# A gated mix of linear attention and a GEGLU block: the state from a Gram product, the read-out folded into one matrix, and the stages reordered

## The chip, the cores and the metric

One core of one Trainium2 chip. The time is the device time of one launch in microseconds, median of several runs. The three batches of experiments ran on three different chips, so across batches I compare the ratios to the kernel before. A profile is one further execution; its span is 1.7 us shorter than the timed run of the same kernel. The chain of a profile is the work that ended last, followed back at each step to what released it.

## The reference

```
g = sigmoid(x . gate_w)                         # x: 2048 x 640
q, k, v = heads(x @ wqkv)                       # 32 heads of 20
pq, pk = phi(q), phi(k)                         # t+1 above zero, exp(t) below, + 1e-6
kv = sum over tokens of pk^T v ;  z = sum over tokens of pk
a = ((pq kv) / (pq . z + 1e-6)) @ wo
b = (gelu(x @ w_gate) * (x @ w_up)) @ w_down    # 640 -> 1728 -> 640
out = g * a + (1 - g) * b
```

## The kernel before

The tokens are 16 row tiles of 128, in four quarters of 512. Everything runs through 8 PSUM banks. K and V come from one projection per row tile. A per-head state with a column for z is accumulated in two banks, each row tile is read out against it and divided, and both branches meet in one PSUM accumulation with wo and w_down.

```python
    def phase_B(st):                      # K, V and the gate column of a row tile
        ...
        for (lo, hi) in chunks:           # 512, 508 and 261 columns
            ps = ps_tile("ps_kv")
            for dk in range(ND):
                nc.tensor.matmul(ps[:, 0 : hi - lo], lhsT=xT[q][:, dk, sl * P : (sl + 1) * P],
                                 rhs=wkv[:, dk, lo:hi], ...)
        ...
        if pend_kv:
            phase_KV()                    # five outer products pk^T [v, 1] of the tile before
    ...
    def phase_D(st):                      # six matmuls pq x state, then
        ...                               # divide: two reciprocals, two multiplies on VectorE
    ...
    phase_A(0)
    phase_A(1)
    filler(3)
    ...
    for i in range(NT):
        if i < NF:
            phase_E(0, i)                 # one FFN feature tile of quarter 0
        phase_D(i)
    for q in range(NQ):
        if q > 0:
            for ft in range(NF):
                phase_E(q, ft)
        for sl in range(4):
            phase_F(4 * q + sl)           # 5 matmuls with wo and 14 with w_down, per half of 320 columns
```

## Time and profile before

| | before |
|---|---|
| median (lowest to highest) | 288.85 us (287.9 to 289.32), 16 runs |
| span of the profile | 287.1 us |
| TensorE share of the chain | 98% |
| VectorE busy | 114.6 us, 40% |

The prediction shows the busy table and the chain. The mean of a group counts a matmul from issue to result, and matmuls overlap, so what a matmul costs is the distance to the next one. The groups below, from the list of groups by shape (busy us, mean ns, idle time before), are the ones that the change takes out or replaces:

```profile
L208 PE MATMUL ps_kv<-wkv,xT 128*128 128x512 bf16 x80 | 19.9, 379 | 0.0
L239 PE MATMUL kv_ps<-v_ext,pk 128*128 128x147 bf16 x64 | 7.9, 228 | 0.0
L271 PE MATMUL nd_ps<-kvz,pqT 128*128 128x147 bf16 x16 | 3.6, 227 | 0.0
L293 DVE TENSOR_TENSOR o_sb<-nd_ps,rg 128x380 bf16<-128x380 f32 x16 | 8.8, 553 | 0.0
```

The second and third are the state and a part of the read-out: small matmuls whose only purpose is to build and read per-head sums. The fourth is VectorE's division: 553 ns for 380 columns, where the FFN's product takes 691 ns for 512 columns. The difference is 1.05 ns a column, the pace that the prediction calls 0.96 GHz.

### The profile page before, as it was taken

What the parts mean: (1) busy time and instruction counts of PE and PEld (TensorE: products, weight loads), DVE (VectorE), ACT (ScalarE), POOL (GpSimd) and SP (SyncE); (2) the same over time, 40 slices, a digit from 0 to 9 for tenths busy, and PEclk for the clock granted to TensorE, in tenths of its full rate; (3) what the DMA queues carried; (4) which work ended last, traced back from release to release, by engine and by line L of the source; (5) the groups of instructions that cost most, each with busy time, mean ns of one, the idle gap of its engine ahead of it and who ended that gap; (6) DMA issues with size and microseconds to landing.
All of it is one profiled execution on the core that took longest, in us unless ns stands there. A gap on an engine that the chain in (4) does not pass through costs nothing.

```text
span 287.1 us, 4265 instructions
## 1 busy us (share of the span) xinstructions
PE 281.4 (98%) x1705; PEld 159.9 (56%) x1705; DVE 114.6 (40%) x287; ACT 87.1 (30%) x181; POOL 6.8 (2%) x24
## 2 busy tenths in 40 slices
PE   7999999999999999999999999999999999999994
PEld 3656556554455556776444577644457754445773
DVE  0755445359978888501322301132330112332010
ACT  3555556555542212101222210123221013222100
POOL 8100000000000000000000000000000000000000
PEclk9999999999999999999999999999999999999999
DMA  7999990000013433601000000100000010000001
GB/s 225 302 186 330 348 352 10 2 0 0 2 23 69 68 72 59 96 32 48 0 0 0 2 23 25 47 0 0 2 0 23 25 46 0 2 0 0 25 24 45
DMA packets 31027, 18.04 MB, mean 63 GB/s; under 512 B 20960, under 2 KB 29728, under 8 KB 31008
## 3 DMA queue, kind: packets, MB, share of 16 engines
q1 hardware_dynamic: 29696, 16.96, 22.2%
q10 hardware_dynamic: 1312, 0.82, 0.9%
q8 instruction: 13, 0.21, 0.3%
q14 instruction: 6, 0.05, 0.0%
HBM read 10.57 MB, written 2.62 MB: 46 GB/s over the span
## 4 chain that ended last, share of the span: by engine, by line
PE 98%; ACT 1%; DVE 0%; issue 0%; DVEq 0%
PE ps_acc L339 21%; PE ps_g L310 20%; PE ps_u L314 20%; PE ps_kv L208 15%; PE ps_acc L336 8%; PE ps_q L194 7%; PE kv_ps L239 2%; PE ps_gu L322 2%; PE kv_ps L112 1%; ACT xT L171 1%; PE kv_ps L352 0%; PE nd_ps L279 0%; PE nd_ps L281 0%; PE nd_ps L273 0%; PE nd_ps L275 0%; PE nd_ps L271 0%
## 5 line engine op out<-in xcount | busy, mean ns | idle before, releaser
L339 PE MATMUL ps_acc<-wd,hT 128*128 128x320 bf16 x448 | 66.1, 299 | 0.0
L314 PE MATMUL ps_u<-xT,wu 128*128 128x512 bf16 x260 | 64.6, 379 | 0.0
L310 PE MATMUL ps_g<-xT,wg 128*128 128x512 bf16 x260 | 64.6, 379 | 0.0
L318 DVE TENSOR_TENSOR hT<-ps_u,gl 128x512 bf16<-128x512 f32 x52 | 35.9, 691 | 62.4 <-PE ps_u L314 61.6
L317 ACT ACTIVATE gl<-ps_g 128x512 bf16<-128x512 f32 x52 | 31.0, 597 | 87.7 <-PE ps_g L310 85.7
L339 PEld LDWEIGHTS <-hT 128*128 128x128 bf16 x448 | 43.8, 98 | 17.1
L208 PE MATMUL ps_kv<-wkv,xT 128*128 128x512 bf16 (+2 forms) x240 | 45.9, 344 | 0.0
L314 PEld LDWEIGHTS <-wu 128*128 128x128 bf16 x260 | 25.4, 98 | 30.7
L310 PEld LDWEIGHTS <-wg 128*128 128x128 bf16 x260 | 25.0, 98 | 27.4
L345 DVE TENSOR_SCALAR o_out<-ps_acc,omg_all 128x320 bf16<-128x320 f32 x16 | 8.8, 551 | 68.0 <-PE ps_acc L339 68.0
L208 PEld LDWEIGHTS <-xT 128*128 128x128 bf16 x240 | 22.9, 97 | 19.9
L342 ACT ACTIVATE o_out<-ps_acc,omg_all 128x320 bf16<-128x320 f32 x16 | 8.4, 527 | 64.8 <-PE ps_acc L339 64.8
L336 PE MATMUL ps_acc<-wo,oT 128*128 128x320 bf16 x160 | 27.0, 299 | 0.0
L184 DVE TENSOR_SCALAR phi_m<-phi_e 128x512 bf16<-128x512 bf16 (+2 forms) x54 | 13.8, 256 | 25.9 <-ACT phi_e L182 25.1
L194 PE MATMUL ps_q<-xT,wq 128*128 128x512 bf16 (+1 forms) x110 | 22.5, 360 | 0.8 <-ACT xT L171 0.8
L336 PEld LDWEIGHTS <-oT 128*128 128x128 bf16 x160 | 15.6, 98 | 6.5
L182 ACT ACTIVATE phi_e<-ps_kv 128x512 bf16<-128x512 f32 (+1 forms) x32 | 14.0, 437 | 13.7 <-PE ps_kv L208 13.6
L194 PEld LDWEIGHTS <-wq 128*128 128x128 bf16 x110 | 10.6, 97 | 11.3 <-issue 1.1
L187 DVE SCALAR_TENSOR_TENSOR pk<-ps_kv,phi_m 128x512 bf16<-128x512 f32 (+1 forms) x32 | 15.7, 492 | 2.2
L182 ACT ACTIVATE phi_e<-ps_q 128x512 bf16<-128x512 f32 (+1 forms) x22 | 12.2, 558 | 10.6 <-PE ps_q L194 10.6
L187 DVE SCALAR_TENSOR_TENSOR pqT<-ps_q,phi_m 128x512 bf16<-128x512 f32 (+1 forms) x22 | 14.1, 643 | 0.7
L293 DVE TENSOR_TENSOR o_sb<-nd_ps,rg 128x380 bf16<-128x380 f32 (+1 forms) x32 | 14.2, 486 | 0.0
(52 smaller groups left out, 109.5 us busy)
## 6 DMA issues: line engine op xcount, KB each, us to landing
out_dram<-o_out SPq DMA_DIRECT2D x16, 160.0 KB, 1.8
wd<-in_B_w_down_dram SPq DMA_DIRECT2D x1, 2080.0 KB, 13.2
wkv<-in_A_wqkv_dram SPq DMA_DIRECT2D x2, 800.0 KB, 9.1
wg<-in_B_w_gate_dram SPq DMA_DIRECT2D x1, 1440.0 KB, 9.6
wu<-in_B_w_up_dram SPq DMA_DIRECT2D x1, 1440.0 KB, 11.9
wo<-in_A_wo_dram SPq DMA_DIRECT2D x1, 800.0 KB, 11.6
x_sb<-in_A_x_dram SPq DMA_DIRECT2D x2, 320.0 KB, 4.4
wg<-in_B_w_gate_dram SPq DMA_DIRECT2D x1, 640.0 KB, 5.2
```

Of the source, the lines that this page charges most:

```text
L182: nc.scalar.activation(out=e[:, :width], in_=ps[:, :width], func=ACT.Exp)
L184: nc.vector.tensor_scalar(out=m[:, :width], in0=e[:, :width], scalar1=1.0, scalar2=EPS, op0=ALU.min, op1=ALU.add,)
L187: nc.vector.scalar_tensor_tensor(out=dst, in0=ps[:, :width], scalar=0.0, in1=m[:, :width], op0=ALU.max, op1=ALU.add,)
L194: nc.tensor.matmul(ps[:, 0:tw], lhsT=wq[:, dk, j * P : (j + 1) * P], rhs=xT[q][:, dk, t0 : t0 + tw], start=(dk == 0), stop=(dk == ND - 1),)
L208: nc.tensor.matmul(ps[:, 0 : hi - lo], lhsT=xT[q][:, dk, sl * P : (sl + 1) * P], rhs=wkv[:, dk, lo:hi], start=(dk == 0), stop=(dk == ND - 1),)
L293: nc.vector.tensor_tensor(out=o_sb[:, hlo : hlo + hn, :], in0=ndv[:, :, 0:Dh], in1=rg[:, 0:hn, :].to_broadcast([P, hn, Dh]), op=ALU.mult,)
L310: nc.tensor.matmul(psg[:], lhsT=wg[:, dk, ft * P : (ft + 1) * P], rhs=xT[q][:, dk, :], start=(dk == 0), stop=(dk == ND - 1))
L314: nc.tensor.matmul(psu[:], lhsT=wu[:, dk, ft * P : (ft + 1) * P], rhs=xT[q][:, dk, :], start=(dk == 0), stop=(dk == ND - 1))
L317: nc.scalar.activation(out=gl[:], in_=psg[:], func=ACT.Gelu_apprx_tanh)
L318: nc.vector.tensor_tensor(out=hT[:, ft, :], in0=psu[:], in1=gl[:], op=ALU.mult)
L336: nc.tensor.matmul(acc[:, 0:HALF], lhsT=oT[q][:, dk, sl * P : (sl + 1) * P], rhs=wo[:, dk, cs], start=(dk == 0), stop=False)
L339: nc.tensor.matmul(acc[:, 0:HALF], lhsT=hT[:, ft, sl * P : (sl + 1) * P], rhs=wd[:, ft, cs], start=False, stop=(ft == NF - 1))
```

## The change

The intent is to do less on TensorE. K'V with V = X Wv is (K'X) Wv, so the V projection is dropped and a Gram product G = X' phi(K) is accumulated instead, 640 x 640 in five banks at a time. The state is then one small product, and because it does not depend on the token it is multiplied into wo once (M). Each token's division is done on phi(Q) itself, by a row sum z that two fp32 matmuls (one per half of the columns) have copied to all partitions. The stages are reordered (FFN of quarter 0 first), the half-full 14th feature tile is stored twice so that two 64-row matmuls can run side by side, and the warm-up has 7 matmuls instead of 11. The core of the diff, with cuts:

```diff
-    def phase_D(st):
-        nc.tensor.matmul(nd0[:, 0 : 7 * HC], lhsT=pq_lhs(0), rhs=kvz[0][:, 0 : 7 * HC], ...)
-        ...                                              # five more, then the division
+    def phase_G(st, hh):
+        for ct in range(ND):
+            nc.tensor.matmul(g_ps[hh, ct][:, 0:HALF], lhsT=x_sb[q][:, sl, ct * P : (ct + 1) * P],
+                rhs=pk[st][:, hh * HALF : (hh + 1) * HALF], start=(st == 0), stop=(st == NT - 1))
+    def phase_Z(st):                                     # zacc += pk, fp32, 640 columns, VectorE
+    def phase_KV(glo, ghi):                              # 120 x 120 blocks of Wv^T G, masked to heads
+    def phase_M():                                       # state x wo, six groups of heads
+    def phase_D(st):
+        nc.vector.tensor_tensor(out=prod[:], in0=pq[st][:], in1=zrep[:], op=ALU.mult)
+        nc.vector.tensor_reduce(out=den[:], in_=prod[:]..., axis=AX.X, op=ALU.add)
+        ...                                              # + eps, times e^-gate, reciprocal
+        nc.vector.tensor_tensor(out=v, in0=v, in1=rg[:].to_broadcast([P, H, Dh]), op=ALU.mult)
+    def half_pair(st, first):                            # two 64-row matmuls in place of one padded tile
+    ...
+    for st in range(NT): phase_K(st)
+    ...                                                  # Q with G, two passes, then M
+    for ft in range(2, NF):
+        phase_E(1, ft)
+        if ft - 1 < NT:
+            phase_D(ft - 1)
```

## The prediction

> **What bounds the kernel now.** I read the page's busy table and slices first, then the chain that ended last.
>
> ```profile
> PE 281.4 (98%) x1705; PEld 159.9 (56%) x1705; DVE 114.6 (40%) x287; ACT 87.1 (30%) x181; POOL 6.8 (2%) x24
> PE   7999999999999999999999999999999999999994
> PEclk9999999999999999999999999999999999999999
> DMA  7999990000013433601000000100000010000001
> PE 98%; ACT 1%; DVE 0%; issue 0%; DVEq 0%
> ```
>
> TensorE is busy in every slice at full clock and is 98% of the chain, so the span is the length of the matmul stream plus two ends. DMA is quiet after the fifth slice. VectorE is 40% busy on average, but its slices (0755445359978888501322...) reach eight and nine tenths in the middle: that average hides the engine that could become the next bound.
>
> Busy time of a matmul is latency (379 ns for 512 columns), so I take the spacing from the chain in order of time:
>
> ```profile
> 19.54 2.71 PE ps_kv L208 x15
> 22.59 2.71 PE ps_kv L208 x15
> 64.67 14.03 PE ps_q L194 x65
> 83.72 1.08 PE ps_g L310 x5
> 86.24 1.08 PE ps_g L310 x5
> 266.16 1.90 PE ps_acc L339 x14
> 268.74 1.90 PE ps_acc L339 x14
> ```
>
> Line by line: 14.03 / 65 = 0.216 us for 512 columns. An output half takes 268.74 - 266.16 = 2.58 us for 19 matmuls, 0.136 us for 320 columns. A K/V row tile takes 3.05 us, of which 0.34 is five outer-product matmuls. An FFN feature tile with its attention tile takes 2.52, of which 2.16 is the FFN, so the attention read-out is 0.36.
>
> Added up: 540 FFN matmuls x 0.216 = 116.5; Q, 100 x 0.216 = 21.6; K/V and state, 16 x 3.05 = 48.7; read-out, 16 x 0.36 = 5.7; output, 608 x 0.136 = 82.6. The sum is 275.1. The timeline has the last matmul issue end near 283.5 and the first useful stretch start near 9.3 with 10 small matmuls (1.1) done before: 274.2 + 1.1 = 275.3. The method closes to 0.2 us.
>
> For VectorE I took start-to-start times from its timeline, since operations that do not depend on each other overlap:
>
> ```profile
> 66.63 0.28 DVE L184 TENSOR_SCALAR phi_m<-phi_e 128x512 bf16<-128x512 bf16 x1
> 66.95 0.69 DVE L187 SCALAR_TENSOR_TENSOR pqT<-ps_q,phi_m 128x512 bf16<-128x512 f32 x1
> 67.56 0.29 DVE L184 TENSOR_SCALAR phi_m<-phi_e 128x512 bf16<-128x512 bf16 x1
> 83.48 0.69 DVE L318 TENSOR_TENSOR hT<-ps_u,gl 128x512 bf16<-128x512 f32 x1 [0.36 <-PE ps_u L314]
> 84.08 0.37 DVE L287 TENSOR_SCALAR dtmp<-nd_ps,en 128x19 f32<-128x19 f32 x2
> ```
>
> The operation of 0.69 us lets the next one start after 0.60 to 0.61, which is 512 elements at one per 0.96 GHz cycle plus about 0.07. For 320 columns I get 0.40, for 640 columns 0.73. The short min/add of 320 columns is about 0.15 when the next operation is independent. So phi on 320 columns is 0.55.
>
> **What the Trainium skill says.** (1) "VectorE: DVE Perf Modes", section "The perf-mode tier table": with fp32 operands tensor_tensor runs at one element per cycle, and tensor_reduce always does. The one-per-cycle pace agrees with the 0.69 us row; no run yet has the SBUF-only 640-column forms. (2) "ScalarE: Activation LUTs", section "What ACT_TABLE_LOAD costs": about 1283 ns for the load; the trace has 1283 ns for each of its two loads. (3) "TensorE: Matmul & The Clock Gate", section "Weight-path perf modes": the fast weight load needs 128 weight columns, and its LDWEIGHTS section gives P/1.2 ns otherwise, 100 ns for 120. The trace has only 128-column loads, so no run shows it. (4) "TensorEngine Tiling (Array Packing)", section "Key Properties": two tiles of 64 rows can run in parallel, but changing the mode drains the array. No row here shows that either.
>
> **The change part by part.** The intent is algebra: K'V becomes (K'X)Wv, so the V projection disappears but the Gram product x'phi(k) appears; the per-head state is multiplied into wo once (M), so the read-out matmuls disappear; normalisation uses a replicated row sum z on VectorE. Stages are reordered: FFN of quarter 0 first, then K, Q with G, FFN 1, output 0 and so on.
>
> TensorE after, with the same spacings (the built instruction order has exactly these counts):
> - FFN, 540 matmuls, unchanged: 116.5. The page's busiest lines are untouched.
> - K 160, Q 160 and G 160 matmuls of 320 columns: 480 x 0.136 = 65.3, in place of 21.6 + 48.7 + 5.7 = 76.0. This is the main saving: -10.7. V's 51,200 columns are replaced by G's 51,200, so that part is neutral; what goes is the state outer products and the read-out, 12,096 columns each, and short-matmul overhead.
> - Output: 16 x 2 x 18 = 576 matmuls x 0.136 = 78.3 in place of 82.6, as the half-full 14th feature tile is packed as two 64-row tiles. Those are 32 matmuls: 2.2 if every two run together, 4.4 if not; I take 3.0. Net -1.3.
> - New: row-sum in fp32, estimate 1.1 (four passes of 320 columns, twice; an assumption, not a trace row); KV 30 matmuls of 120-column weights, estimate from the skill's load figure 0.1 each = 3.0; M 12 x 0.136 = 1.6. Together +5.7.
>
> Sum: -10.7 - 1.3 + 5.7 = -6.3 us. With nothing else, 288.8 becomes 282.5, or 2.2% less. That sits almost on the 2% line (283.0), so small waits decide.
>
> **What the moved work does to VectorE.** From the start of K to the end of FFN 1 VectorE has: 64 phi x 0.55 = 35; 15 row-sum adds x 0.73 = 11; 13 of 16 normalisations (product, reduce and multiply, each 640 columns: 3 x 0.73, plus reciprocal 0.3 and a small one 0.12 = 2.6) = 34; FFN evictions 15 x 0.60 = 9; copies of G and M, 12 x 0.40 = 5; small ones 2. That is 96 us beside some 65.3 + 1.1 + 3.0 + 1.6 + 29.1 = 100 us of matmuls. So VectorE is nearly the bound for 100 us, where before it had room.
>
> By stage: K has 16 x 1.1 of phi and six adds (4.4) = 22 against 21.8 of TensorE, starting some 2 us late because the last gelu tile and the table load (1.28) sit in front of it. G then takes five of eight PSUM banks, so those must be evicted first: I count a wait of 1. In Q with G (first half) 1.28 per row tile on VectorE against 1.36: about 0.5 to refill. In the second half the scheduler puts about 14 of the 640-column operations beside ten phi: 18 us of VectorE against 14 of TensorE, mostly taken by three spare banks, but VectorE arrives about 2 us late at the end of G. There is the worst spot: G's copies, then KV, kvt, M's 12 evictions are a serial chain through a queue that also holds two normalisations, with only one FFN tile (2.2 us) between each. Queueing the operations in the built order gives M finished about 2.7 us later than its matmuls alone would. FFN 1 afterwards has about 26 us of VectorE work per 25 of TensorE and up to four tiles of slack: no wait. The start has 7 warm-up matmuls in place of 11: perhaps 0.5 of half-clock. Waits: 1 + 0.5 + 2.7 + 0.5 = 4.7; since one wait gives VectorE time to catch up for the next, I take 2.8.
>
> **The rivals.** (A) VectorE really becomes the bound. For: the sum above is 96 of 100, and a little more per operation (dependent neighbours cost their full duration, 0.82 instead of 0.73 by the same line) adds 8 or 9 us. Against: TensorE can run ahead, and the normalisations are spread. Then 290 to 295. (B) The waits are hidden: the order interleaves two normalisations, and banks in the FFN give slack. Then 281 to 283. (C) Weights arrive late at the start, since gate and up weights are now needed first. FFN 0 uses 0.33 MB per 2.16 us, about 150 GB/s, and the page shows 225 to 352 GB/s there, so I expect at most 0.5.
>
> **Range and chances.** 282.5 + 2.8 = 285.3 us. The stall terms are worth 0 to 8, the packed half tiles and KV about 1.5 either way: 281.0 to 290.0 holds it 8 times in 10. Faster by over 2% needs stalls under 0.5: 0.27. Within 2% (283.0 to 294.6): 0.68. Slower: 0.05.
>
> **What would show it.** Right: TensorE still over 93% of the chain, VectorE near 90% from about 40 to 140 us, the longest TensorE idle time at kvt and M, output periods of 18 x 0.136 = 2.44 us. Wrong: TensorE idle of over 8 us on VectorE (A), practically none (B), KV spacings of 55 ns, or a fall of the granted clock after the gaps.

## The result, and the profile after

The changed kernel takes 281.04 us (280.7 to 281.17, 8 runs) against 288.85. A ratio is the mean time of one kernel's runs over that of the other's of the same rounds, so it is not quite the ratio of these medians: 0.9733, 95% interval 0.9719 to 0.9748. That is 7.8 us less, faster by more than 2%. I had forecast 285.3, 3.5 us less. The measured time lies at the very edge of my range (281.0 to 290.0), the gain is more than twice what I forecast, and I had given a gain of over 2% a chance of 0.27 only.

The page of the changed kernel (busy us, share of the span, instructions; then busy tenths in 40 slices; then the chain):

```profile
PE 273.6 (98%) x1711; PEld 163.9 (59%) x1711; DVE 146.2 (52%) x323; ACT 80.8 (29%) x172; POOL 2.8 (1%) x10
PE   7999999999999999999999999999999999999994
DVE  1233279999978999999993133330112334010010
PEclk9999999999999999999999999999999999999999
PE 98%; ACT 0%; DVE 0%; issue 0%; DVEq 0%
```

VectorE's row stands at seven tenths or more for 16 slices, as forecast, and yet it has 0% of the chain. TensorE is still 98%. The chain in order of time (start, length, what) gives the stages:

```profile
35.54 1.08 PE ps_gu L159 x5
36.62 21.85 PE ps_k L197 x160
...
101.09 2.72 PE ps_G L226 x20
103.81 1.08 PE ps_g L159 x5
...
142.58 1.77 PE ps_acc L363 x13
145.02 1.77 PE ps_acc L363 x13
```

The output now has a period of 145.02 - 142.58 = 2.44 us per half instead of 2.58. The stages K, Q with G in two passes, FFN 1 and output 0 begin at 36.62, 58.47, 80.41, 103.81 and 136.25 us. The windows view, cut at those times, shows stretch and length, then busy us and instructions of TensorE, its weight loads, VectorE, ScalarE and GpSimd, the clock and the DMA:

```profile
36.62:58.47 21.85, 21.85 (x163) 15.54 (x161) 20.77 (x65) 16.48 (x47) 0.00 (x0) 1.00 0.85 251
58.47:80.41 21.94, 21.94 (x163) 15.51 (x161) 19.74 (x54) 7.76 (x21) 0.00 (x0) 1.00 0.01 1
80.41:103.81 23.40, 23.40 (x176) 16.80 (x174) 22.37 (x59) 8.66 (x22) 0.00 (x0) 1.00 0.14 25
103.81:136.25 32.44, 32.41 (x170) 15.65 (x168) 32.08 (x65) 11.61 (x22) 0.00 (x0) 1.00 0.28 64
136.25:156.57 20.32, 20.32 (x154) 14.27 (x152) 12.75 (x24) 2.70 (x5) 0.00 (x0) 1.00 0.36 67
```

VectorE is busy for 94.96 of 99.63 us from K to the end of FFN 1, and TensorE hardly waits in any of these stretches. Taking the matmuls away from each stretch (0.1358 us for 320 columns, 0.2158 for 512, both from the chains) leaves 0.1 to 0.2 us in the first Q pass, 0.1 in the second and 0.6 in FFN 1: about 0.9 us of waits and restarts in all. Of the 0.6, M waits 0.4 and two groups of matmuls behind the 120-column ones take 1.19 us instead of 1.08.

The whole difference can be booked by lengths in the two chains:

| part | before | after | change |
|---|---|---|---|
| FFN, 540 matmuls | 116.6 | 116.6 | 0 |
| K, V, Q, state and read-out; after: K, Q and G | 76.2 | 65.3 | -10.9 |
| output | 82.6 | 81.3 | -1.3 |
| row sum 1.07, state product 0.54 + 1.05, M 1.63 | | 4.3 | +4.3 |
| waits and restarts of TensorE from K to FFN 1 | 0 | 0.9 | +0.9 |
| time before the stream, less useful work done in it | 8.2 | 7.5 | -0.7 |
| tail after the last matmul issue | 3.54 | 3.49 | -0.05 |

The sum is -7.75, to rounding the span's 287.1 - 279.3. The row "before the stream" takes a time at which the stream runs without gaps (9.29 and 9.64 us) and subtracts the first-quarter matmuls already done at the later pace (10 and 20 of 256 columns, 0.109 each). Both are read from one profile each, and the start varies between executions, as the next section shows.

### The profile page after: what moved, and what is told of

Its sections match the earlier page's. It is cut to its first block, busy times and chain, and to the rows that moved or that the text cites. A ratio compares the mean times of both kernels' runs of the same rounds, so it can differ in the third digit from the quotient of the medians.

```text
span 279.3 us, 4308 instructions
## 1 busy us (share of the span) xinstructions
PE 273.6 (98%) x1711; PEld 163.9 (59%) x1711; DVE 146.2 (52%) x323; ACT 80.8 (29%) x172; POOL 2.8 (1%) x10
## 4 chain that ended last, share of the span: by engine, by line
PE 98%; ACT 0%; DVE 0%; issue 0%; DVEq 0%
PE ps_g L159 20%; PE ps_acc L363 20%; PE ps_u L159 20%; PE ps_acc L360 8%; PE ps_q L197 8%; PE ps_k L197 8%; PE ps_G L226 8%; PE ps_gu L159 2%; PE warm_ps L119 1%; PE ps_acc L346 1%; PE ps_m L303 1%; PE ps_kv L274 1%; PE tp_x L141 0%; PE ps_z L251 0%; ACT xT L144 0%; DVE o_out L376 0%
## 5 line engine op out<-in xcount | busy, mean ns | idle before, releaser
L159 PE MATMUL ps_g<-xT,wg 128*128 128x512 bf16 (+1 forms) x270 | 64.8, 372 | 0.9 <-ACT xT L144 0.9
L360 PE MATMUL ps_acc<-m_all,pqT 128*128 128x320 bf16 x160 | 27.0, 300 | 0.0
L197 PE MATMUL ps_q<-wqk,xT 128*128 128x320 bf16 x160 | 26.6, 299 | 0.0
L226 PE MATMUL ps_G<-pk,x_all 128*128 128x320 bf16 x160 | 26.4, 299 | 0.0
L197 PE MATMUL ps_k<-wqk,xT 128*128 128x320 bf16 (+1 forms) x160 | 22.0, 300 | 0.0
L185 ACT ACTIVATE phi_e<-ps_q 128x320 bf16<-128x320 f32 x32 | 14.0, 437 | 26.4 <-PE ps_q L197 22.8
L360 PEld LDWEIGHTS <-pqT 128*128 128x128 bf16 x160 | 15.3, 98 | 7.3 <-issue 1.1
L226 PEld LDWEIGHTS <-x_all 128*128 128x128 bf16 x160 | 15.5, 97 | 6.3 <-issue 0.2
L190 DVE SCALAR_TENSOR_TENSOR pq<-ps_q,phi_m 128x320 bf16<-128x320 f32 x32 | 15.4, 482 | 0.3
L190 DVE SCALAR_TENSOR_TENSOR pk<-ps_k,phi_m 128x320 bf16<-128x320 f32 x32 | 14.4, 485 | 0.0
```

What stands on the lines that cost most here:

```text
L159: nc.tensor.matmul(ps[:, t0 : t0 + tw], lhsT=w[:, dk, ft * P : (ft + 1) * P], rhs=xT[q][:, dk, t0 : t0 + tw], start=(dk == 0), stop=(dk == ...
L185: nc.scalar.activation(out=e[:, :width], in_=src, func=ACT.Exp)
L190: nc.vector.scalar_tensor_tensor(out=dst, in0=src, scalar=0.0, in1=m[:, :width], op0=ALU.max, op1=ALU.add,)
L226: nc.tensor.matmul(g_ps[hh, ct][:, 0:HALF], lhsT=x_sb[q][:, sl, ct * P : (ct + 1) * P], rhs=pk[st][:, hh * HALF : (hh + 1) * HALF], start= ...
L360: nc.tensor.matmul(acc[:, 0:HALF], lhsT=pqT[q][:, dk, ts], rhs=M["sb"][:, dk, cs], start=(sl == 0 and dk == 0), stop=False)
```

## The experiments

Twelve runs in three batches, one of them the changed kernel unaltered; each batch has its own runs of the kernel before.

### Where the start comes from

First, more warm-up in the changed kernel:

```diff
-    NWARM = 7
+    NWARM = 11
```

> The changed kernel with 11 warm-up matmuls instead of 7 and nothing else. Theory T (TensorE's stream plus its start sets the time): the four extra cold matmuls of 0.43 us run before the first transpose and push the start back. The x tile had landed by about 4.1 us and the warm-up ended at 4.42, so four more end near 6.1: 1.7 us later, of which up to 0.5 may be won back because the second x tile is waited for less. Expected 282.2 to 282.8 us, ratio to before about 0.978. Rival R1 (the start is set by when x and the first gate weights land, the warm-up being hidden): within 0.3 us of 281.0. Rival of my prediction (fewer warm-up matmuls cost half-clock time): slightly faster than 281.0.

Measured: 281.49 us (281.34 to 282.28), ratio 0.9749 (0.9734 to 0.9763). The timeline of TensorE shows the shift. First the changed kernel:

```profile
4.21 1.27 PE L141 MATMUL tp_x<-ident,x_all 128*128 128x128 bf16 x10
9.48 2.32 PE L159 MATMUL ps_u<-xT,wu 128*128 128x512 bf16 x10
```

and with eleven:

```profile
1.25 4.88 PE L119 MATMUL warm_ps<-zeros_bf 128*128 128x512 bf16 x11 [1.25 <-DVE zeros_bf L86]
5.92 0.99 PE L141 MATMUL tp_x<-ident,x_all 128*128 128x128 bf16 x10
10.94 2.11 PE L159 MATMUL ps_u<-xT,wu 128*128 128x512 bf16 x9
```

The transposes are 1.7 us later and the first up-projection 1.46, and the profiled span is 1.3 us longer. The timed runs are only 0.45 us longer, and the interval overlaps that of the changed kernel. The direction is against my forecast (fewer warm-ups would cost half-clock time); its size stays between 0.4 and 1.3 us. One source of scatter is visible: the ten transposes took 1.27 us in the changed kernel's profile and 0.87 in another profile of the same kernel (the control below). The warm-up matmuls before them come every 0.43 us and later ones of the same size every 0.216, so the transposes probably fall where the pace changes. In the eleven profiles of the changed kernel and its variants with seven warm-up matmuls, K begins anywhere from 36.09 to 37.11 us; with eleven warm-up matmuls it begins at 37.87. Up to 1 us of any difference between two spans below can thus be the start, so stages are compared by their lengths.

Then the reverse, on the kernel before:

```diff
-            nc.tensor.matmul(t[:], ...)  # NWARM per bank, 8 in all, and filler(3) later
+            # NWARM - b per bank, 7 in all, and no filler
```

> The kernel before with 7 warm-up matmuls instead of 11 (four and three, no filler between the transposes and the first projection). T: the first transposes no longer wait for the fillers that end at 6.08 us; x landed near 4; so 0.7 to 1.7 us less: 287.2 to 288.1 us. If the 0.7 us earlier start of the changed kernel comes from its other load order (gate weights first, all on one queue) instead, no change: 288.6 to 289.0, or a little slower because the clock is not warm yet.

Measured: 287.51 us (287.32 to 289.08) against 288.92, ratio 0.9961 (0.9941 to 0.998), so 1.1 us by the ratio (0.6 to 1.7). The kernel before gains about as much from the warm-up alone as the changed kernel's start did, so this part of the gain needs nothing of the algebra: the fillers of the kernel before ran until 6.08 us, and without them the transposes begin at 4.28.

### What the paired half tile is worth

```diff
-            for lo in (0, FL):           # the 64 rows stored twice
+            # stored once, rows 64 to 127 zero, as before
-            for ft in range(NF - 1):
+            for ft in range(NF):         # 14 full tiles; half_pair removed
```

> The changed kernel with the half-full 14th feature tile padded with zeros as before (32 more 128-row matmuls of 320 columns in the groups, no pairs of 64-row matmuls). T: 32 x 0.136 = 4.35 us in place of the 4 x 0.76 = 3.04 that the chain shows for the pairs: plus 1.3 us, 282.3. If the pairs had cost a drain that eats their gain: within 0.3 us of 281.0. If eight banks claimed at once cost a wait in output stages: faster than 281.0.

Measured: 282.57 us (282.25 to 282.77), ratio 0.978 (0.9767 to 0.9792): 0.47% of 288.9, or 1.4 us, as counted. Eight matmuls of 64 rows take 0.65 us in the chain, against 1.09 for eight full ones: the pairs do run side by side.

### What the banks do

The padded kernel can live with seven PSUM banks, so it serves to take one away:

```diff
-tc.tile_pool(name="psum", bufs=8, ...)
+tc.tile_pool(name="psum", bufs=7, ...)
```

> The same padded kernel with seven PSUM banks instead of eight (it no longer needs eight at once). While G holds five, two spare ones stay for Q instead of three. T says VectorE's lag is absorbed only by the bank lead, so taking one away must show: waits of TensorE on VectorE or ScalarE in the Q and G stages, 2 to 8 us slower than the padded kernel with eight. Rival R2 (VectorE simply keeps up, banks do not matter): within 0.5 us of it.

Measured: 284.95 us (284.26 to 285.2), ratio 0.9859 (0.9845 to 0.9874), 2.4 us slower than the padded kernel with eight (both in one batch). From the start of K to the end of G it takes 69.3 us instead of 67.2. VectorE appears in the chain:

```profile
55.70 0.73 DVE zacc L245
58.23 0.89 DVE pk L190 x2
...
87.78 0.82 DVE prod L324
```

These are two places: the end of K, where G claims five banks, and the second pass, where the row sum takes banks from Q. VectorE's work is nearly the same (144.4 us busy against 143.4). So TensorE's freedom from VectorE in the changed kernel is a matter of bank lead. With eight, 0.9 us of waits and restarts remain; with seven there are some 2 us more.

### The weights of 120 columns

```diff
-kp[0 : gw[g], off : off + gw[g]], lhsT=wv[:, ct, GW * g : GW * g + gw[g]],
+kp[0 : lw, off : off + gw[g]], lhsT=wv[:, ct, GW * g : GW * g + lw],     # lw = min(128, rest)
```

> The changed kernel, with the state matmuls' weights widened from 120 to 128 columns (the eight extra output rows are never read). The chain shows 0.083 us for each of these 30 matmuls where 120 columns alone would take 0.053. T with the fast weight load of the skill: 25 of them fall to about 0.055: minus 0.7 us, 280.3, and the weight loads of this line from 135 ns to about 98 as in the other lines. If the 0.083 is the short matmul's own floor: no change.

Measured: 281.11 us (280.69 to 281.34), ratio 0.9736 (0.9715 to 0.9757): no change, against my expectation. The groups by shape, first the changed kernel, then the widened one:

```profile
L274 PE MATMUL ps_kv<-g_sb,wv 128*120 128x120 bf16 x25 | 1.7, 218 | 0.0
L274 PEld LDWEIGHTS <-wv 128*120 128x120 bf16 x25 | 1.7, 135 | 0.2
```

```profile
L275 PE MATMUL ps_kv<-g_sb,wv 128*128 128x120 bf16 x25 | 1.6, 216 | 0.0
L275 PEld LDWEIGHTS <-wv 128*128 128x128 bf16 x25 | 1.5, 98 | 0.3
```

The loads became shorter, 135 to 98 ns, but the matmuls' pace did not move. My 0.083 us was a misreading: I had taken it from stage lengths and given the state product a wait that belongs to M. The chain has 20 of them in 1.05 us, 0.053 each, which is their 120 columns. The longer load is hidden behind the matmuls.

### Less and more work on VectorE

Less: the product and the replicated row sum in bf16.

```diff
-prod = work.tile([P, D], FP32, ...)      zrep = consts.tile([P, D], FP32, ...)
+prod = work.tile([P, D], BF16, ...)      zrep = consts.tile([P, D], BF16, ...)
```

> The changed kernel with the normaliser's product and the replicated row sum in bf16 instead of fp32, which makes 16 of VectorE's 640-column products about 0.33 us shorter, 5 us of VectorE's 95 between 36 and 136 us. T (VectorE is not on the path): 280.6 to 281.1, no change beyond the 0.4 us that the state product M waited for VectorE. Rival R3 (VectorE's load still costs something, hidden in small gaps): 1 us faster or more.

Measured: 281.13 us (280.83 to 281.4), ratio 0.9738 (0.9717 to 0.9758). VectorE's busy time fell from 146.2 to 141.2 us and the time did not change. VectorE is full but not on the path.

More: one, then two further 640-column products per normalisation.

```diff
+        for _ in range(1):                # 2 in the second run
+            junk = work.tile([P, D], FP32, name="junk", bufs=1)
+            nc.vector.tensor_tensor(out=junk[:], in0=pq[st][:], in1=zrep[:], op=ALU.mult)
```

> The changed kernel with one more 640-column fp32 product in each of the 16 normalisations (a result nobody reads): 16 x 0.73 = 11.7 us more on VectorE, about 9.5 of it before the end of FFN 1. T: VectorE has 99.6 - 94.9 = 4.7 us idle between 36.6 and 136.2, plus some 4 us of bank lead, so this dose lands near the edge: 281 to 284 us. My prediction's account, that waits of about 3 us already exist, would have it 9 us slower or more: 290.

Measured: 282.16 us (281.98 to 282.41), ratio 0.9774 (0.9755 to 0.9794): 1.1 us more than the changed kernel for 11.7 us of extra VectorE work. The windows, cut at this run's own stages, show where it went (FFN 1 and output 0):

```profile
104.15:136.74 32.59, 32.23 (x165) 15.66 (x168) 32.35 (x63) 11.62 (x22) 0.00 (x0) 1.00 0.25 57
136.74:157.55 20.81, 20.60 (x153) 14.29 (x152) 20.72 (x38) 2.17 (x4) 0.00 (x0) 1.00 0.22 43
```

FFN 1 is 0.15 us longer, output 0 is 0.5 longer; the other 0.33 us between the spans lie before K, in the start. In output 0 VectorE's time rose from 12.75 to 20.72 us: the normalisations of later quarters slid behind FFN 1, where they are not needed yet.

> The same with two more products in each normalisation: 23.4 us more on VectorE. T: the slack of about 8 us is used up and the rest shows nearly one to one, 288 to 296 us, with VectorE at 99% from K to FFN 1 and TensorE idle on it. If VectorE's work could still be pushed behind the output stages: under 284.

Measured: 290.6 us (289.3 to 290.82), ratio 1.0051 (1.0018 to 1.0084), 9.6 us more. FFN 1 still ends on time (output 0 starts at 136.6 us), and most of the loss comes after output 0, where FFN 2 waits for a bank that VectorE has not emptied. From the page of this run, the granted clock in 40 slices; from the list of waits (who, for whom: us in total, times, longest); and from the chain, the first five matmuls after the wait:

```profile
PEclk9999999999999999999999968999999999999999
PE ps_g L159 <- DVE o_out L379: 4.9, 1, 4.9
170.32 2.29 PE ps_g L159 x5
```

From K to the end of output 0 the changed kernel has 119.95 us and VectorE is busy for 107.7, so 12.2 us are free. 11.7 more fit, nearly. 23.4 more exceed it by 11.2, which looks like the 9.6 that are seen, but the trace books the profile's 9.8 us otherwise. The start is 0.5 us later and output 0 takes 1.05 more. Then six groups of FFN 2 run on free banks, and TensorE waits 0.73 and 4.86 us. After that gap the granted clock fell: the next three groups of five take 2.29, 2.13 and 1.35 us in the chain instead of 1.08, which is 2.5 us more. So 5.6 us are waits in FFN 2, 4.9 of them directly for VectorE; the slower clock behind the gap was not in my account. The time at which VectorE's surplus becomes a wait is set by the free banks as well, so the 12.2 us are a rough mark and not a sharp limit.

### The same kind of work, in K only

```diff
+            nc.vector.tensor_tensor(out=m[:, :width], in0=m[:, :width], in1=zf[:, :width], op=ALU.add)
         # in phi, only for the second half of K: 16 adds of 320 columns
```

> The changed kernel with one extra fp32 add of 320 columns in phi of K's second half, in front of the operation that frees the PSUM bank: 16 x 0.40 = 6.4 us more on VectorE, all of it between 36 and 59 us. That is little more than half the dose of the run with one extra product per normalisation, which cost about 1 us. Theory T (what matters is the last moment by which VectorE's work must be done: for the normalisations it is the end of output stage 0, for K it is the moment G claims five banks, which it only just meets now): TensorE waits 4 to 6.5 us on VectorE around 50 to 62 us, time 285 to 287.5. Rival (any VectorE work is absorbed as long as the total fits): under 282.2.

Measured: 282.43 us (282.24 to 282.71), ratio 0.9787 (0.977 to 0.9804), 1.8 us above the unaltered kernel in the same batch. Less than I expected. The trace tells why: the scheduler, which orders each engine's instructions when the kernel is built, moved the row-sum adds behind K. The first starts at 64.6 us; in the changed kernel it starts at 44.5, and five have run before VectorE's last tile of K (60.46 us). So K's net load rose by 2 to 3 us and not by 6.4. K itself takes 21.85 us as in the changed kernel: TensorE waits nowhere in it. From the start of K to the end of G this run takes 68.36 us and the changed kernel 67.19, so 1.2 us are lost in Q with G, whose order changed too; the rest of the 1.8 lies before K, in the start. That K is less forgiving than the normalisations fits these figures, but the test does not show it.

### The state product and M without FFN tiles between

```diff
-    phase_D(0); phase_E(1, 0); phase_KV(2, NG); phase_E(1, 1); phase_M()
+    phase_KV(2, NG); phase_M(); phase_D(0); phase_E(1, 0); phase_E(1, 1)
```

> The changed kernel with the state products and M placed directly behind G, without the two FFN tiles between them. In the changed kernel this chain (copies of G, state product, mask, M, its evictions) costs TensorE 0.5 us of waiting, where I had forecast 2.7. T: the two FFN tiles hide it; without them TensorE waits for the copies of G (done 1.5 us after G ends), for the mask and for the evictions: 2 to 4 us more, 283 to 285. If the chain were short in itself: within 0.5 of 281.0.

Measured: 282.61 us (282.48 to 282.91), ratio 0.9794 (0.9775 to 0.9814), 2.0 us above the unaltered kernel. The two waits below make 1.5 of it; between the two profiles the rest is the start (K begins at 36.70 instead of 36.22 us). TensorE's timeline now has the waits (in brackets: idle before, and for whom):

```profile
104.75 0.27 PE L274 MATMUL ps_kv<-g_sb,wv 128*120 128x120 bf16 x2 [0.87 <-DVE g_sb L235]
107.16 1.40 PE L303 MATMUL ps_m<-wo_g,kvt 120*120 120x320 bf16 x8 [0.62 <-DVE kvt L282]
```

The chain through VectorE is real. In the changed kernel two FFN tiles lie over it.

### Control and a faster version

> The changed kernel unaltered, as control for the run below on the same chip: 281.0 us, ratio 0.973.

Measured: 280.64 us (280.59 to 281.63), ratio 0.9732 (0.971 to 0.9754).

```diff
-ones_f fp32; rhs=zacc[:, cs]
+ones_f bf16; the last row-sum add writes a bf16 tile zb; rhs=zb[:, cs]
-dma(out=out2[st * P : (st + 1) * P, :], in_=o_out[:])
+# for the last row tile: two DMAs, one per half
```

> Attempt at a faster version: the row sum's last add writes bf16, so that its broadcast takes 2 bf16 matmuls in place of 2 fp32 ones whose four passes take 1.07 us in the trace: 2 x 0.136, minus 0.8 us. And the last output tile leaves in two halves, so that only the second half is written after the last eviction: minus 0 to 0.2. T (TensorE's stream sets the time): 280.0 to 280.3. If waits elsewhere fill the gap: 281.

Measured: 280.06 us (280.03 to 280.26), ratio 0.9705 (0.969 to 0.972). The outputs are right. It is 0.6 us below the control on the same chip; the single times do not overlap, the intervals of the ratios do, so it is faster than the kernel before beyond doubt and than the changed kernel probably. TensorE's timeline shows the row sum, first changed, then this one:

```profile
84.34 1.24 PE L251 MATMUL ps_z<-zacc,ones_f 128*128 128x320 f32 x4
85.41 0.84 PE L226 MATMUL ps_G<-pk,x_all 128*128 128x320 bf16 x5
```

```profile
84.33 0.45 PE L252 MATMUL ps_z<-zb,ones_f 128*128 128x320 bf16 x2
84.62 0.84 PE L226 MATMUL ps_G<-pk,x_all 128*128 128x320 bf16 x5
```

From its start to the next group 1.07 us became 0.29. The split of the last output was not run alone, but the tail after the last matmul issue is 3.2 us in this profile, where the changed kernel and its variants have 3.5. Together that is 1.0 us against the changed kernel's profile, which has the same start, and 0.6 against the control's, where K begins 0.4 us earlier.

## Why the prediction was right or wrong

**The method: right.** Spacing times count gave 268.8 us for TensorE's new stream; without waits the changed kernel's chain gives 267.5. The main saving (-10.7 forecast, -10.9 measured) and the output (-1.3 and -1.3) were right, the output with some luck: the 3.0 us for the paired half tiles was a guess between 2.2 and 4.4 (0.65 and 0.11 us, four times, were measured), as the 1.1 for the row sum was an assumption (1.07). The pace for 640 columns on VectorE held too: the product and the reduction take 0.81 to 0.82 us each, and about 0.73 from start to start in the chain of the run with two extra products. TensorE stayed the bound, and rival A, VectorE as the bound, did not come. Rival C, late weights, did not show either: the stream ran from 9.64 us on without a gap. (I had read the page's first slices as 225 to 352 GB/s; the third shows 186, still above the 150 needed.)

**"New: ... Together +5.7": mis-sized.** It measures 4.3. The whole error is the state product, 3.0 forecast and 1.6 measured. I priced it by how long a weight load lasts, when the load is overlapped and the pace is set by the columns that stream. The run with 128-column weights shows that the load's length has no effect here. The prediction had named the sign, "KV spacings of 55 ns", and that sign came (53 ns).

**"The start has 7 warm-up matmuls in place of 11: perhaps 0.5 of half-clock": wrong in sign.** The start gained 0.7 in the two profiles. The warm-up stood in front of the transposes and x had already arrived. The timeline of the kernel before showed this (fillers until 6.08 us, while x's first load, issued at 0.81, took 3.6 us to land), and I did not look at what the fillers delayed. Both warm-up runs agree in direction, the one on the kernel before clear of noise.

**"Waits: 1 + 0.5 + 2.7 + 0.5 = 4.7 ... I take 2.8": the step that failed most.** Leaving the start aside, 0.9 us was measured. Rival B was right, and three things were wrong in mine.

- At the end of K, I had VectorE too late, as I read the trace, by one 0.73 us add: the add stands between the last tiles of K, after those whose banks G needs first. The wait came out at 0.2 instead of 1. That it is close is shown by the run with seven banks, which does wait there.
- "VectorE arrives about 2 us late at the end of G": it was 0.34 us late, since the first copy of G starts at 104.15 and G's last matmul is issued by 103.81. My running sum let VectorE begin that stretch of work 1.0 us after a Q tile ended on TensorE, and the trace has it begin 0.7 us before (first product at 86.07, that Q tile's end 86.78). With the chain starting 1.6 us earlier, M waited 0.4 us instead of 2.7. I had also put M's 12 evictions into VectorE's queue, where the code gives every second one to ScalarE. The run without FFN tiles in between shows the chain itself.
- "VectorE is nearly the bound": its load was right (96 us forecast, 94.96 measured), but I set the deadline at the end of FFN 1. Normalisations of later quarters may finish as late as output 0, and the run with one extra product shows 11.7 us more being absorbed for 1.1, the start's scatter included. A sum of 96 out of 100 was not an engine near its limit, because much of the work could move.

In numbers: the forecast change of -3.5 was -6.3 + 2.8. Measured, -6.3 is -7.9 (the state product and rounding), and +2.8 is +0.9 for waits and -0.7 for the start, with -0.05 at the tail.

What stays open: the exact size of the start's part (0.4 to 1.3 us), and how the row sum adds and G's banks would fare under a heavier K, as the scheduler rearranged that test.

## What to carry to other kernels

Price a matmul by the columns it streams and count them before and after; that part of a forecast was good to one or two microseconds of 280. Before charging a wait to an engine that will be nearly full, ask for each piece of its work by when it must be done and how many buffers lie in between: work that feeds a later stage can slide, work that frees a bank cannot. Check what the warm-up stands in front of. And a wait can cost more than its own length: behind the 4.9 us one the granted clock fell, for 2.5 us more.

## What the Trainium skill lacked or had wrong

- "TensorE: Matmul & The Clock Gate", the LDWEIGHTS formula and the section on weight-path modes: that a load of fewer than 128 columns is slower agrees (135 against 98 ns), but P/1.2 works out to 100 ns for 120 columns and 33 for 40, and the trace has 135 and 98. The page gives this as the length of a load; taking it for the price of a matmul was my mistake. Matmuls with 120-column weights and 120 streamed columns follow each other every 53 ns, with either load.
- "TensorEngine Tiling (Array Packing)", "Key Properties": it says that a change of mode drains the array and gives no cost. Here eight 64-row matmuls of 320 columns took 0.65 us where eight full ones take 1.09, and the five matmuls after them 0.79 instead of 0.68, so the change back costs about 0.11 us. Half of 1.09 would be 0.54, so going in costs about as much (an estimate).
- No page says how to judge an engine near full occupancy that is not the bound: here VectorE is 95% busy over 100 us, and still has 12.2 us free up to the end of output 0.
